# Sums of weights from the first down projection on, and the scores' biases on VectorE

## The chip, the cores and the metric

The kernel runs on one core of a Trainium2 chip. Its time is the device time of one execution in microseconds; the number compared is the median over runs. One further execution of the kernel was taken with a profiler; its trace is what the profile's rows come from.

The engines are named as in the profile: PE is TensorE (matmuls), PEld its loads of weights, DVE is VectorE, ACT is ScalarE, POOL is GpSimd, SP is SyncE, which here only issues DMAs. Each engine works through its own list of instructions in order.

## The reference: what is computed

The inputs are q, k and v of 8 batches, 8 heads, 576 positions and 64 columns in float32, and three weights. First comes attention with a window of 128 positions and a bias that falls with distance; then, for the 4608 rows of its output, two products with weights of 512 x 1536, multiplied element by element, and a product with a weight of 1536 x 512:

```python
scores = np.where(mask, scale * q @ k.T + bias, -1e9)   # mask: 0 <= rel < 128
attn = softmax(scores)
x = (attn @ v) laid out as (4608, 512)
a = x @ w_a
b = x @ w_b
out = (a * b) @ w_out
```

## The kernel before

**Precision.** Nearly every float32 operand is split into a high and a low float16 part, scaled by a power of two. A product is then three float16 matmuls (high x high, high x low, low x high). `wup` holds the split parts of the two up weights, `wdn` those of the down weight, `xs` those of a batch's x, `h` those of the hidden values.

**Batches.** The work goes by batch (0 to 7). While TensorE does the up projection (`up`, or `first_up` for batch 0) and the down projection (`down`, or `first_down`) of batch b, the attention of batch b+1 is worked through beside it. `attention()` is a generator; `Pace.along` moves it on by a share with each step of the projection, so its place is tied to the projection's steps. Attention goes by pairs of heads: load and split q and k, four banks of scores (`scores`: matmuls, an addition of the bias with its row minimum on VectorE at line 388, an exponential on ScalarE at 389), normalisation (405, 406), a transpose by DMA (411), the product with v (507).

**Plain and fast units.** The up projection of a batch goes by 12 units f of 128 hidden columns. A *plain* unit (`up_plain`) makes four results (two weights, two halves of the positions), each from two terms of 6 matmuls: 48 matmuls of 288 columns. A *fast* unit (`up_fast`) gets the same from seven products of 6 matmuls, 42 in all, after the scheme of Strassen and Winograd. It needs sums of blocks of x, and sums of blocks of the weights. `ways` says for each batch which units are plain, which come first, and which are fast. Before, batches 0 and 1 are all plain, batch 2 has 6 plain units, batch 3 has 2, and the others none.

The evictions differ too. A plain unit copies two results (ScalarE, 867) and multiplies two (VectorE, 869). A fast unit has three on ScalarE (881, 893, 899), four on VectorE (888, 904, 909, 916) and a multiplication on GpSimd (911). Both then split the hidden values (`halve`, 848 and 849).

**Sums of x.** `split_x(st, plain, fast)` splits the blocks of a batch's x, a copy on ScalarE (441) and a subtraction on VectorE (442) for each. Plain units need four blocks. Fast ones need seven, four of them after a subtraction on GpSimd (455, 458, 460, 465). A batch with both needs eight.

**Sums of weights.** `sums_of_weights()` is a generator of 25 steps. Each of the first 24 takes one half of one unit's weights: five additions on GpSimd (248 to 252). The next step commits it: two copies on ScalarE (258) and two subtractions on VectorE (260) into `wup` and `wsum`. Its scratch is unused room in `wsum` for units 0 to 7, and for units 8 to 11 it takes two of the four buffers `t` that the scores use as well. The first addition is ordered behind the last bias (`issue_after(last_bias[0].ins)`), the copies behind the last eviction of a projection. `quota` says how many steps are taken beside which steps of a batch's up and down projection. Before: 9 and 4 in batch 1, 3 and 5 in batch 2, and 4 in the down projection of batch 3. `weave` takes them in equal distances.

**The bias.** `before_scores` makes, for each pair of heads, a tile of 128 x 192: distances times the pair's scale and the heads' slopes, one `tensor_scalar` on GpSimd (365). There is one such buffer, so it is written when the pair before has read it for the last time (388).

**Order.** In the part with batch 0 the order on all engines but SyncE, and from batch 1 on the order on all engines but TensorE, is laid down beforehand by a scheduler that simulates the kernel, with earlier statements first where several are ready; `high_priority` moves the evictions up. From batch 1 on TensorE's order is that of the program.

Of the kernel before, what the change touches and what calls it, by code (L numbers as in the profile page):

```python
# [18 lines left out]
ALU = mybir.AluOpType  # L19
# [27 lines left out]
def attention_then_bilinear_ffn(ctx: ExitStack, tc: tile.TileContext, qT, kT, vP, w_a, w_b, w_out, rel, slopes2, outT):  # L47
# [187 lines left out]
    def sums_of_weights():  # L235


        spare = cycle([flat[:, n:n + 4 * P].rearrange("p (s f) -> p s f", s=4) for n in range(8 * 6 * P, 12 * 6 * P, 4 * P)])

        def place():  # L240
            return next(spare) if f < 8 else work.tile([P, 4, P], F32, tag="t", name="ws32", bufs=4)

        late = []
        for f, k in [(f, k) for f in range(NF) for k in range(2)] + [(None, None)] * 1:
            if f is not None:
                a, z = place(), place()
                with tc.issue_after(last_bias[0].ins):
                    pool.tensor_tensor(out=a, in0=wup[:, f, 0:4, 0, k, :], in1=wup[:, f, 0:4, 1, k, :], op=ALU.add)
                pool.tensor_tensor(out=z[:, 0, :], in0=a[:, 3, :], in1=a[:, 2, :], op=ALU.add)
                pool.tensor_tensor(out=z[:, 2, :], in0=a[:, 0, :], in1=a[:, 3, :], op=ALU.subtract)  # L250
                pool.tensor_tensor(out=z[:, 1, :], in0=z[:, 0, :], in1=a[:, 0, :], op=ALU.subtract)
                pool.tensor_tensor(out=z[:, 3, :], in0=a[:, 1, :], in1=z[:, 1, :], op=ALU.subtract)
            late.append((f, k, z))
            if len(late) > 1:
                g, m, x = late.pop(0)
                with tc.issue_after(last_main[0].ins):
                    for w, z in ((wup[:, g, 3:4], x[:, 0:1, :]), (wsum[:, g], x[:, 1:4, :])):
                        act.copy(w[:, :, 0, m, :], z)
                for w, z in ((wup[:, g, 3:4], x[:, 0:1, :]), (wsum[:, g], x[:, 1:4, :])):
                    vec.tensor_tensor(out=w[:, :, 1, m, :], in0=z, in1=w[:, :, 0, m, :], op=ALU.subtract)  # L260
            yield
# [100 lines left out]

    def before_scores(o, ninv):
        o.bias = work.tile([P, WIN], F32, tag="bias", name="bias")
        last_bias[0] = pool.tensor_scalar(out=o.bias, in0=rel_sb, scalar1=ninv, scalar2=sl2_sb[:, o.p:o.p + 1], op0=ALU.mult, op1=ALU.mult)  # L365
        o.mn, o.sm, o.rin = (small.tile([P, 9], F32, tag=tag, name=tag) for tag in ("mn", "sm", "rin"))
        o.n, o.parts = 0, []

# [298 lines left out]
    def attention():  # L667
# [34 lines left out]
        for i in range(n + 1):  # L702
# [53 lines left out]
            if prev and p == 0:  # L756
                states[b - 1] = st
                assert started["down"] == b - 2
                for k, _ in enumerate(split_x(st, b - 1 <= 3, b - 1 >= 2)):
                    yield i + (4.2 + 0.2 * k) / 7  # L760
            yield i + 5 / 7
            if o:
# [13 lines left out]
            prev, o = o, nxt  # L776
            yield i + 1

    states, started, first_reads, last_read, last_main, last_bias = {}, {"down": -1}, [None], [None], [None], [None]


    def new_hidden():
# [227 lines left out]


    every = list(range(NF))
    ways = [(every, [])] * 2 + [(every[6:], every[:6]), (every[10:], every[:10])] + [([], every)] * (B - 4)
    att = Pace(attention())
    spread = sums_of_weights()

    quota = [((), ()), (((8, 48, 9),), ((0, 48, 4),)), (((0, 24, 3),), ((0, 48, 5),)), ((), ((0, 48, 4),))] + [((), ())] * (B - 4)

    def first_batch():
        st = states[0]  # L1020
        weave(att.along(first_up(st, h), 49, 3.2), (weights, 0, 40, 50))
        weave(att.along(first_down(0, out_scale(st), h), 24, 5.15), (weights, 0, 12, 12))
        for _ in weights:
            pass

# [55 lines left out]
```

## Time and profile before

| | us |
|---|---|
| median of 3 runs | 991.28 (991.03 to 994.67) |
| the profiled execution | 989.81 |
| its span, first to last instruction | 988.0 |
| TensorE busy | 962.1 |
| VectorE busy | 669.0 |
| ScalarE busy | 635.6 |
| GpSimd busy | 255.3 |

The span is cut by the profiler from the first to the last instruction; the execution's own time has 1.8 us more around it. Busy time is the union of an engine's instructions. The granted clock of TensorE is 0.995 in the mean. The rows of the groups give, after the shapes and the count, the busy time in us, the mean of one instruction in ns, and the idle time of the engine before them with what ended it. In a row of the timeline the idle time and its releaser stand in brackets.

### The profile page before, as it was taken

To read this page: it belongs to the slowest core of one execution; us is meant where nothing else is said; L and a number is where in the kernel's file an instruction comes from. 1 tells how busy PE (TensorE), PEld (TensorE's weight loads), DVE (VectorE), ACT (ScalarE), POOL (GpSimd) and SP (SyncE) were. 2 spreads that over 40 slices of the span, in tenths; PEclk is the share of its full clock that TensorE was granted. 3 is DMA by queue.
4 is the path that set the end of the run, shared out by engine and by line. 5 is a ranking of instruction groups with operands and counts; after the bars stand their busy time and mean duration, and the time that the engine had idled before them with its cause. 6 is when DMAs were issued, how large, how long until landed. Compare 5 with 4: busy or idle time off the path is not lost.

```text
span 988.0 us, 23867 instructions
## 1 busy us (share of the span) xinstructions
PE 962.1 (97%) x9339; PEld 748.9 (76%) x9339; DVE 669.0 (68%) x1867; ACT 635.6 (64%) x1729; POOL 255.3 (26%) x309
## 2 busy tenths in 40 slices
PE   7899999999999999999999999999999999999998
PEld 5567777677777777777777777777777777877776
DVE  5979998668688657777778677757776576514520
ACT  5977769667676667766767766777667766413321
POOL 1211122032546313541225222211232012311100
PEclk8999999999999999999999999999999999999999
DMA  8434753664337234463345362373245432200001
GB/s 333 168 126 172 231 154 67 151 158 92 80 74 183 68 69 87 107 172 75 68 92 121 120 118 65 87 191 84 59 84 117 133 74 38 55 34 5 1 13 36
DMA packets 148432, 102.82 MB, mean 104 GB/s; under 512 B 120032, under 2 KB 128352, under 8 KB 147296
## 3 DMA queue, kind: packets, MB, share of 16 engines
q1 hardware_dynamic: 138816, 91.77, 38.2%
q10 hardware_dynamic: 9504, 9.54, 3.0%
q8 instruction: 73, 1.20, 0.5%
q14 instruction: 39, 0.32, 0.1%
HBM read 48.33 MB, written 9.44 MB: 58 GB/s over the span
## 4 chain that ended last, share of the span: by engine, by line
PE 69%; DVE 12%; ACT 7%; DMA 7%; issue 3%; POOL 1%; SPq 0%; ACTq 0%; DVEq 0%
PE ch L856 19%; PE dn_ps L952 18%; PE p L856 14%; PE up_ps L856 9%; PE x_ps L507 4%; DMA v<-in_vP 4%; PE sc_ps L384 3%; DVE phl L406 2%; PE dn_ps L818 2%; ACT t L389 1%; DVE wsum L135 1%; DVE xs L442 1%; ACT phl L405 1%; DVE wsum L134 1%; DMA qk<-in_kT 1%
## 5 line engine op out<-in xcount | busy, mean ns | idle before, releaser
L856 PEld LDWEIGHTS <-wup 128*128 128x128 f16 x3072 | 296.3, 98 | 82.0 <-issue 5.7
L952 PE MATMUL dn_ps<-h,wdn 128*128 128x288 f16 x2016 | 254.4, 286 | 0.0
L952 PEld LDWEIGHTS <-wdn 128*128 128x128 f16 x2016 | 193.9, 98 | 52.0 <-issue 0.2
L856 PE MATMUL up_ps<-xs,wup 128*128 128x288 f16 x1536 | 194.6, 286 | 1.1 <-ACT rc L867 0.8
L856 PEld LDWEIGHTS <-wsum 128*128 128x128 f16 x1152 | 111.7, 98 | 32.0 <-issue 2.5
L911 POOL TENSOR_TENSOR rc<-rc,row 128x288 f32<-128x288 f32 x64 | 62.3, 974 | 279.8 <-DVE row L909 263.9
L389 ACT ACTIVATE t<-t,mn 128x192 f32<-128x192 f32 (+2 forms) x252 | 107.2, 427 | 24.5 <-DVE mn L388 24.4
L856 PE MATMUL ch<-xs,wup 128*128 128x288 f16 x768 | 115.0, 286 | 0.5 <-ACT row L893 0.5
L856 PE MATMUL p<-xs,wup 128*128 128x288 f16 x768 | 115.1, 286 | 0.0
L406 DVE SCALAR_TENSOR_TENSOR phl<-t,rin,phl 128x192 f16<-128x192 f32 (+2 forms) x252 | 104.6, 454 | 15.3 <-ACT phl L405 15.1
L856 PE MATMUL ch<-xs,wsum 128*128 128x288 f16 x768 | 111.5, 286 | 1.1 <-ACT rc L881 1.1
L848 ACT CAST h<-rc 128x576 f16<-128x576 f32 x96 | 64.1, 668 | 69.1 <-DVE rc L916 37.2
L405 ACT ACTIVATE phl<-t,rin 128x192 f16<-128x192 f32 (+2 forms) x252 | 88.9, 425 | 25.3 <-DMA pT<-phl 12.7
L849 DVE TENSOR_TENSOR h<-rc,h 128x576 f16<-128x576 f32 x90 | 69.5, 772 | 30.5 <-ACT h L848 29.7
L388 DVE CUSTOM_DVE_ANT_0 t<-sc_ps,bias,neg 128x192 f32<-128x192 f32 (+2 forms) x216 | 73.9, 389 | 7.6 <-PE sc_ps L384 7.5
L957 ACT ACTIVATE row<-dn_ps,oi 128x288 f32<-128x288 f32 x56 | 27.6, 493 | 55.9 <-PE dn_ps L952 55.9
L893 ACT ACTIVATE row<-ch,g 128x288 f32<-128x288 f32 x64 | 31.8, 497 | 48.9 <-PE ch L856 48.9
L442 DVE TENSOR_TENSOR xs<-v,xs 128x576 f16<-128x576 f32 x52 | 47.8, 935 | 21.4 <-ACT xs L441 21.3
L888 DVE TENSOR_TENSOR rc<-p,rc 128x288 f32<-128x288 f32 x64 | 29.1, 454 | 44.3 <-PE p L856 34.7
L365 POOL TENSOR_SCALAR bias<-rel_sb,ninv,sl_sb 128x192 f32<-128x192 f32 x24 | 20.0, 832 | 147.8 <-DVE mn L388 129.8
L856 PE MATMUL p<-xs,wsum 128*128 128x288 f16 x384 | 57.5, 286 | 0.0
L436 POOL TENSOR_TENSOR xq<-xq,sq 128x576 bf16<-128x576 bf16 x22 | 29.2, 1325 | 75.7 <-ACT sq L435 75.7
(155 smaller groups left out, 1386.1 us busy)
## 6 DMA issues: line engine op xcount, KB each, us to landing
v<-in_vP SPq DMA_DIRECT2D x8, 1280.0 KB, 6.2
out<-row ACTq DMA_DIRECT2D x62, 144.0 KB, 1.8
qk<-in_qT SPq DMA_DIRECT2D x28, 288.0 KB, 4.0
qk<-in_kT SPq DMA_DIRECT2D x28, 288.0 KB, 4.4
wdn<-in_w_a SPq DMA_DIRECT2D x12, 512.0 KB, 5.1
wdn<-in_w_b SPq DMA_DIRECT2D x12, 512.0 KB, 6.1
wdn<-in_w_out SPq DMA_DIRECT2D x12, 512.0 KB, 4.6
qst<-qkh SPq DMA_DIRECT2D x24, 144.0 KB, 2.7
```

Source lines behind the costliest of these rows:

```text
L388: vec.tensor_tensor_reduce(out=t[:, c:c + w], in0=ps[:, c:c + w], in1=o.bias[:, WIN - w:WIN], scale=-0.125 if o.b == 1 else o.neg, scalar= ...
L389: act.activation(t[:, c:c + w], t[:, c:c + w], AF.Exp, bias=o.mn[:, n:n + 1], scale=-1.0, accum_out=o.sm[:, n:n + 1])
L405: act.activation(phl[:, 0, pc:pc + w], e, AF.Copy, scale=s)
L406: vec.scalar_tensor_tensor(out=phl[:, 1, pc:pc + w], in0=e, scalar=s, in1=phl[:, 0, pc:pc + w], op0=ALU.mult, op1=ALU.subtract)
L442: vec.tensor_tensor(out=xs[:, n, 1, :, :], in0=src, in1=xs[:, n, 0, :, :], op=ALU.subtract)
L507: last = pe.matmul(xp[oc // 512][64 * h:64 * h + 64, o0:o0 + w], vt[0:rows, c:c + 64], probs(pt, rows, blocks, h), start=(n == 0 and first ...
L848: act.copy(h[:, f, :, 0, :], hid)
L849: eng.tensor_tensor(out=h[:, f, :, 1, :], in0=hid, in1=h[:, f, :, 0, :], op=ALU.subtract)
L856: pe.matmul(ps[:, 0:HT], w[:, wi, k, :], xs[:, b, xi, k, :], start=(first and n == 0), stop=(last and n == len(ks) - 1), skip_group_check= ...
L893: last_read[0] = last_main[0] = act.activation(mid, ch, AF.Copy, scale=st.g)
L911: pool.tensor_tensor(out=x0, in0=x0, in1=mid, op=ALU.mult)
L952: pe.matmul(ps[:, 0:HT], wdn[:, f, wi, e * P:(e + 1) * P], h[:, f, t, hi, :], start=(m == 0 and n == 0), stop=(m == NF - 1 and n == 2))
```

## The change

- `ways`: batch 0 stays plain, batch 1 becomes 8 plain and 4 fast units, and all later batches become fast.
- `quota` and the first batch: 9 steps of the sums beside the second half of the first down projection, 10 beside the up projection of batch 1 and 6 beside its down projection. After that there are none.
- `split_x`: batch 1 is split for both kinds (eight blocks), later ones for fast units alone (seven).
- The bias is formed by VectorE. The sums' first addition is no longer ordered behind it.

```diff
@@ sums_of_weights
-                with tc.issue_after(last_bias[0].ins):
-                    pool.tensor_tensor(out=a, in0=wup[:, f, 0:4, 0, k, :], in1=wup[:, f, 0:4, 1, k, :], op=ALU.add)
+                pool.tensor_tensor(out=a, in0=wup[:, f, 0:4, 0, k, :], in1=wup[:, f, 0:4, 1, k, :], op=ALU.add)
@@ before_scores
-        last_bias[0] = pool.tensor_scalar(out=o.bias, in0=rel_sb, scalar1=ninv, scalar2=sl2_sb[:, o.p:o.p + 1], op0=ALU.mult, op1=ALU.mult)
+        vec.tensor_scalar(out=o.bias, in0=rel_sb, scalar1=ninv, scalar2=sl2_sb[:, o.p:o.p + 1], op0=ALU.mult, op1=ALU.mult)
@@ attention
-                for k, _ in enumerate(split_x(st, b - 1 <= 3, b - 1 >= 2)):
+                for k, _ in enumerate(split_x(st, b - 1 <= 1, b - 1 >= 1)):
@@
-    ways = [(every, [])] * 2 + [(every[6:], every[:6]), (every[10:], every[:10])] + [([], every)] * (B - 4)
+    ways = [(every, []), (every[4:], every[:4])] + [([], every)] * (B - 2)
-    quota = [((), ()), (((8, 48, 9),), ((0, 48, 4),)), (((0, 24, 3),), ((0, 48, 5),)), ((), ((0, 48, 4),))] + [((), ())] * (B - 4)
+    quota = [((), ()), (((8, 60, 10),), ((0, 48, 6),))] + [((), ())] * (B - 2)
@@ first_batch
-        weave(att.along(first_down(0, out_scale(st), h), 24, 5.15), (weights, 0, 12, 12))
+        weave(att.along(first_down(0, out_scale(st), h), 24, 5.15), (weights, 0, 12, 12), (spread, 12, 24, 9))
```

More of the change, by code (lines that the diff above doesn't have):

```diff
@@ L777, in attention @@
             yield i + 1
-    states, started, first_reads, last_read, last_main, last_bias = {}, {"down": -1}, [None], [None], [None], [None]
+    states, started, first_reads, last_read, last_main = {}, {"down": -1}, [None], [None], [None]
     def new_hidden():
```

## The prediction

> **What bounds the kernel now.** I read the page first, for the engines and the chain that ended last; then the timeline of TensorE, for where each batch begins and where it stood still; then the groups of instructions by line; then the stretches that the change loads. The page:
>
> ```profile
> PE 962.1 (97%) x9339; PEld 748.9 (76%) x9339; DVE 669.0 (68%) x1867; ACT 635.6 (64%) x1729; POOL 255.3 (26%) x309
> ...
> DVE  5979998668688657777778677757776576514520
> ...
> PE 69%; DVE 12%; ACT 7%; DMA 7%; issue 3%; POOL 1%; SPq 0%; ACTq 0%; DVEq 0%
> ```
>
> TensorE is busy for 97% of the span and makes 69% of the chain. A busy row alone does not say that matmuls run at their rate, so here are two merged rows of the chain, 108 and 288 matmuls of 288 columns end to end:
>
> ```profile
> 326.67 13.25 PE up_ps L856 x108
> ...
> 949.44 35.29 PE dn_ps L952 x288
> ```
>
> 13.25/108 and 35.29/288 are both 0.1225 us: with nothing in the way, that is the price of a matmul. The starts of the up projections of batches 1 to 5 on TensorE's timeline:
>
> ```profile
> 200.33 0.53 PE L856 MATMUL up_ps<-xs,wup 128*128 128x288 f16 x3
> 324.06 0.53 PE L856 MATMUL up_ps<-xs,wup 128*128 128x288 f16 x3
> 441.11 0.53 PE L856 MATMUL up_ps<-xs,wup 128*128 128x288 f16 x3
> 554.80 0.65 PE L856 MATMUL ch<-xs,wup 128*128 128x288 f16 x4
> 667.08 0.53 PE L856 MATMUL ch<-xs,wup 128*128 128x288 f16 x3
> ```
>
> The differences are 123.73, 117.05, 113.69 and 112.28 us for batches 1 to 4. By the lists in the kernel these hold 12, 6, 2 and 0 plain units, and a plain unit has 48 matmuls where a fast one has 42. From batch 2 to batch 4 six units go from plain to fast: 36 x 0.1225 = 4.4 us, and the trace has 4.77. From batch 3 to 4: 12 x 0.1225 = 1.5, and the trace has 1.41. So in this part of the kernel a removed matmul is worth its price. Where TensorE did stand still around the places that the change touches:
>
> ```profile
> 146.32 0.18 PE L103 MATMUL wtot<-c,ones 128*128 128x1 bf16 x1 [2.44 <-DVE c L102]
> ...
> 183.93 1.54 PE L507 MATMUL x_ps<-pT,vhl 128*64 128x128 f16 x42 [2.44 <-DMA pT<-phl]
> ...
> 310.65 0.18 PE L337 MATMUL qtot<-both,ones 128*128 128x2 bf16 x1 [1.17 <-DVE both L329]
> ```
>
> The stalls wait for VectorE at the end of the weights' conversion (146), for the attention's transpose in the first down projection (184), and for VectorE again in batch 1's down projection (311). How full VectorE is there, by stretches (length, then PE, PEld, DVE, ACT and POOL busy):
>
> ```profile
> 80.00:140.00 60.00, 60.00 (x538) 45.96 (x537) 58.97 (x126) 41.62 (x103) 13.25 (x14) 1.00 0.60 186
> ...
> 165.00:200.30 35.30, 32.87 (x362) 25.32 (x360) 19.92 (x66) 21.88 (x62) 4.82 (x5) 1.00 0.69 147
> ...
> 255.00:282.00 27.00, 26.59 (x259) 21.29 (x257) 20.08 (x53) 19.02 (x54) 14.00 (x23) 1.00 0.34 75
> 282.00:311.00 29.00, 27.83 (x292) 21.43 (x290) 24.96 (x72) 20.20 (x60) 15.47 (x16) 1.00 0.48 97
> ```
>
> VectorE is full from 80 to 140 (58.97 of 60), half empty in the first down projection (19.92 of 35.30), at 74% at the end of batch 1's up projection and at 86% right behind it. GpSimd is idle in the first down projection (4.82 of 35.30).
>
> **The change, part by part.** *Matmuls.* Plain units fall from 12 + 6 + 2 = 20 to 8, all in batch 1. Twelve units give up 6 matmuls each: 72 x 0.1225 = **-8.8 us**, of which 24 matmuls in batch 1 (2.9), 36 in batch 2 (4.4) and 12 in batch 3 (1.5). These are on the bounding engine.
>
> *Batches 2 and 3.* They become what batch 4 is, but for the stage of their attention. They lose all of their 12 steps of sums, and split 7 blocks of x instead of 8. By the differences above, the stalls that go beside the matmuls are 4.77 - 4.4 and 1.41 - 1.5, together **-0.3 us** (bounds -1.5 and 0: neither batch can lose more idle time than the 1.17 us kind of stall that the trace shows around them).
>
> *The evictions that a fast unit adds.* Rows of the groups, by line (busy us, mean ns of one):
>
> ```profile
> L869 DVE SCALAR_TENSOR_TENSOR rc<-rc,g,up_ps 128x288 f32<-128x288 f32 x40 | 20.2, 507 | 3.0 <-PE up_ps L856 2.8
> ...
> L888 DVE TENSOR_TENSOR rc<-p,rc 128x288 f32<-128x288 f32 x64 | 29.1, 454 | 44.3 <-PE p L856 34.7 <-ACT rc L881 5.9 <-ACT phl L405 3.4
> L904 DVE TENSOR_TENSOR rc<-ch,rc 128x288 f32<-128x288 f32 x64 | 29.2, 456 | 10.5 <-PE ch L856 10.1
> L909 DVE SCALAR_TENSOR_TENSOR row<-p,g,row 128x288 f32<-128x288 f32 x64 | 32.8, 512 | 6.5 <-PE p L856 6.1
> L916 DVE SCALAR_TENSOR_TENSOR rc<-rc,g,ch 128x288 f32<-128x288 f32 x64 | 32.7, 511 | 23.6 <-PE ch L856 23.4
> L911 POOL TENSOR_TENSOR rc<-rc,row 128x288 f32<-128x288 f32 x64 | 62.3, 974 | 279.8 <-DVE row L909 263.9 <-ACT rc L881 13.2 <-ACT phl L405 2.7
> ```
>
> A plain unit costs VectorE 2 x 0.507 = 1.01 us, a fast one 0.454 + 0.456 + 0.512 + 0.511 = 1.93: 0.92 us more for each of the 12, and GpSimd 0.97 more. In batches 2 and 3 this is the load that batch 4 carries already, behind a full TensorE, so nothing. In batch 1 it is 4 x 0.92 = 3.7 us, all in the last 28 of 60 steps, since plain units come first.
>
> *The sums of weights.* One step is five additions on GpSimd, two copies on ScalarE and two subtractions on VectorE; the views of lines 248, 249 and 260 give min/median/max:
>
> ```profile
> L248 POOL TENSOR_TENSOR wsum<-wup x16: 1149/1160/1667, 213.1 to 357.1; 128x512 f32<-128x512 f16 x16
> L249 POOL TENSOR_TENSOR wsum<-wsum x16: 452/484/1041, 217.0 to 358.4; 128x128 f32<-128x128 f32 x16
> ...
> L260 DVE TENSOR_TENSOR wup<-wsum,wup x16: 277/292/1279, 230.8 to 406.3; 128x128 f16<-128x128 f32 x16
> L260 DVE TENSOR_TENSOR wsum<-wsum x16: 544/558/1503, 231.1 to 406.7; 128x384 f16<-128x384 f32 x16
> ```
>
> With the other three short additions taken as the one shown, a step is 1.16 + 4 x 0.48 = 3.1 us of GpSimd and 0.29 + 0.56 = 0.85 of VectorE. Their number stays 24 (a 25th only commits the last); only the place moves. Nine go into the second half of the first down projection: 28 us of GpSimd, which has 30 idle there, and 7.7 of VectorE, which has 15.4. There too go four more splits of batch 1's x and the four subtractions before them:
>
> ```profile
> L442 DVE TENSOR_TENSOR xs<-v,xs 128x576 f16<-128x576 f32 x52 | 47.8, 935 | 21.4 <-ACT xs L441 21.3
> ...
> L458 POOL TENSOR_TENSOR v<-v 128x576 f32<-128x576 f32 x6 | 8.4, 1408 | 46.4 <-ACT v L420 46.4
> ```
>
> That is 4 x 0.94 = 3.7 us of VectorE and 4 x 1.41 = 5.6 of GpSimd. VectorE then has 19.9 + 7.7 + 3.7 = 31.3 of 35.3 us to do. GpSimd overflows a little into batch 1, which harms nobody: the first fast unit comes behind 32 plain steps of 12 matmuls, 32 x 12 x 0.1225 = 47 us later. What can harm is an in-order queue: the addition of squares (GpSimd), the copies of the commits (ScalarE) and the exponentials stand in one line, and the transpose at 184 is already late. Bounds for this stretch: 0 when the lists slip past each other, and 5 us when half of the 7.7 + 3.7 us of VectorE come ahead of the transpose. I take **+0.7 us**, nearer to nothing because both engines had near half of the stretch free.
>
> *The end of batch 1's up projection* (255 to 282 now). It gets shorter by 24 x 0.1225 = 2.9 us, so 24.1. VectorE has 20.1 now, with three and a half commits; with six it gets 2.5 x 0.85 = 2.1 more, 3.7 for the fast units and 0.4 for a bias: 26.3. That is more than the stretch holds, by 2.2 us, and the next one (24.96 of 29.00, six sums in the whole down projection instead of four, one split fewer) cannot take much of it; its stall at 311 shows that attention had no slack left. Bounds: 0, when the plain stage ahead runs commits early; 6 us, when the 2.2 comes together with the whole 3.7 of the fast units. I take **+1.8 us**.
>
> *The biases.* 28 of them move from GpSimd to VectorE. The trace has no such instruction on VectorE; beside its row on GpSimd stand the nearest ones on VectorE, two scalars on one column, and one scalar on 288 columns out of PSUM:
>
> ```profile
> L365 POOL TENSOR_SCALAR bias<-rel_sb,ninv,sl_sb 128x192 f32<-128x192 f32 x24 | 20.0, 832 | 147.8 <-DVE mn L388 129.8 <-ACT rc L867 18.0
> ...
> L964 DVE TENSOR_SCALAR oi<-g,smin,so 128x1 f32<-128x1 f32 x8 | 2.2, 271 | 0.2
> L823 DVE TENSOR_SCALAR row<-dn_ps,oi 128x288 f32<-128x288 f32 x3 | 1.5, 510 | 0.0
> ```
>
> So between 0.27 and 0.51 us; by width 0.27 + 192/288 x 0.24 = 0.43, and I take 0.41. Most of them lie under a full TensorE. Two do not: this timeline of GpSimd puts two biases into the stretch where VectorE is full and TensorE then waits for it at 146.
>
> ```profile
> 82.64 0.43 POOL L365 TENSOR_SCALAR bias<-rel_sb,sl_sb 128x192 f32<-128x192 f32 x1 [0.30 <-DVE mn L388]
> 112.48 0.86 POOL L365 TENSOR_SCALAR bias<-rel_sb,sl_sb 128x192 f32<-128x192 f32 x1 [0.60 <-DVE mn L388]
> ```
>
> 2 x 0.41 = **+0.8 us** (0.5 to 1.0). What the move frees is GpSimd's queue: its bias had to wait for VectorE's last read of the one bias buffer, and the sums were ordered behind it. On VectorE that wait is the engine's own order. The view of line 365 lists nobody who waited for it, so nothing is gained directly.
>
> *The sum:* -8.8 - 0.3 + 0.7 + 1.8 + 0.8 = -5.8 us. The span of 988.0 becomes 982.2, the profiled execution's 989.81 becomes 984.0. The median of the runs, 991.28, lies 1.5 above that execution; with the same distance I predict **985.5 us**.
>
> **A rule against it.** When VectorE and GpSimd add at the same time, both are slow. VectorE's timeline and GpSimd's at 300, and the group of that VectorE instruction over the whole run:
>
> ```profile
> 300.83 3.64 DVE L406 SCALAR_TENSOR_TENSOR phl<-t,rin,phl 128x192 f16<-128x192 f32 x3 [0.52 <-ACT phl L405]
> ...
> 300.40 2.38 POOL L248 TENSOR_TENSOR wsum<-wup 128x512 f32<-128x512 f16 x2
> ...
> L406 DVE SCALAR_TENSOR_TENSOR phl<-t,rin,phl 128x192 f16<-128x192 f32 x196 | 88.5, 493 | 6.1 <-ACT phl L405 6.0
> ```
>
> Three instructions took 3.64 us, 1.2 each instead of the mean of 0.49, beside two first additions of 1.2 each. The Trainium skill says why (SBUF — State Buffer, Who interferes with whom): the two engines share a pair of ports, held for a whole instruction; a VectorE instruction with two inputs in SBUF, or one such as a scalar operation in its two-port mode, and a GpSimd instruction that reads SBUF wait for each other in full. The two rows agree with it.
>
> **Rivals.** (A) *Forecast*: the matmuls' price less stalls of some 3 us. (B) *Clean saving*: the list order absorbs the three stall terms; -8.8 - 0.3 and half a bias term leave about -8.7, 982.6 us. For it: batches 2 to 4 show the full price. Against: VectorE at 26.3 of 24.1. (C) *Given back*: VectorE becomes the bound from 165 to 311, where sums on GpSimd, now free to run beside everything, stretch VectorE's two-input work as at 300. All 24 first additions would stand there, where 13 stood by `quota`; each of the 11 more costs up to 1.2 - 0.5 = 0.7 us of VectorE's time, 7.7 us. With all of it on the path in place of my 0.7 + 1.8: -8.8 - 0.3 + 0.8 + 7.7 = -0.6, 990.7 us, no change. For it: the rows at 300. Against: it happened at 300 beside a stall of only 1.17 us. By the port rule alone (C) would be the likeliest; I give less, since the same additions run in both kernels. (D) *Slower*: the commits stand on the chain. In first down and batch 1, VectorE and ScalarE run their lists in order, TensorE's order is fixed by hand in batch 1, and a score's product waits at its place. The work added from 165 to 324 is 9 x 0.85 + 4 x 0.94 + 7 x 0.41 + 4 x 0.92 + 3 x 0.85 = 20.5 us of VectorE. If all of it reached TensorE: -8.8 - 0.3 + 0.8 + 20.5 = +12, 1003.5 us. It decides from 13.3 us on the path (two thirds), where the sum is +5. Against: VectorE has 15.4 us free in the first down projection alone. (E) *It doesn't do what it says*: the sums come no earlier, because their copies wait for ScalarE's output evictions, and the first fast unit waits; 47 us of slack speak against it.
>
> **How the numbers follow.** About 0.5% (5 us) is what a measurement of this kernel can tell from no change; the bounds are 986.3 and 996.2. A 0.42 and B 0.16 make faster 0.58. C 0.31 and E 0.03 make no change 0.34. D has 0.08. The range of 8 in 10 is 981.0 (B with 1.5 us of stalls gone) to 991.0 (C). A's own is 982.9 to 987.5.
>
> **What would show it.** Right: line 856 with 72 matmuls fewer; batches 2 and 3 at about 112.3 us each; batch 1 at 122 to 124 us; the up projection of batch 1 starting 1 to 2 us later than 200.33; biases on VectorE at 0.41; GpSimd's sums starting at about 165. Wrong: batch 1 over 128 us, new waits of TensorE at line 337 or 384 on VectorE above 3 us, or batch 1 beginning after 205, would mean (C) or (D). Batch 1 under 121 would mean (B).

## The result: slower by 1.2%, and the profile after

The changed kernel takes **1004.18 us** (median of 6 runs, 1002.91 to 1005.76), beside 992.03 for the kernel before on the same chip (988.85 to 994.67). The ratio is 1.0124, 95% interval 1.0104 to 1.0145. Forecast were 985.5 us and a range up to 991.0: wrong in size and in sign.

The page of the changed kernel, the rows that answer to those of before:

```profile
span 1002.8 us, 23788 instructions
...
PE 957.4 (95%) x9267; PEld 742.8 (74%) x9267; DVE 700.7 (70%) x1921; ACT 642.2 (64%) x1743; POOL 260.6 (26%) x297
...
PE 68%; DVE 16%; DMA 6%; ACT 6%; issue 2%; POOL 0%; SPq 0%; ACTq 0%; DVEq 0%; POOLq 0%
```

And the groups of the biases on VectorE (busy us, mean ns):

```profile
L364 DVE TENSOR_SCALAR bias<-rel_sb,ninv,sl_sb 128x192 f32<-128x192 f32 x24 | 9.8, 407 | 0.2
...
L364 DVE TENSOR_SCALAR bias<-rel_sb,sl_sb 128x192 f32<-128x192 f32 x4 | 1.2, 308 | 0.0
```

Three things are in them. TensorE has 72 matmuls fewer (9339 to 9267), as the lists say, yet its busy time falls by 4.7 us where 72 x 0.1225 = 8.8 were expected. Its idle time rises from 988.0 - 962.1 = 25.9 to 1002.8 - 957.4 = 45.4 us. That is 19.5 us, and 19.5 - 4.7 is the 14.8 us by which the span grew. The missing 4.1 us of busy time fit a lower granted clock: its mean over the span is 0.991, and was 0.995, and 0.4% of 957 us is 3.8. And VectorE is busy for 31.7 us more. The counted work explains 28 biases (11.0 us), twelve fast units at 0.92 (11.0) and two more splits at 0.94 (1.9), together 23.9; the count of instructions fits as well (28 + 24 + 2 = 54 = 1921 - 1867). The other **7.8 us belong to no added instruction**: existing ones got longer. VectorE's share of the chain rose from 12 to 16%.

Where the time went by batch, from TensorE's timeline of the changed kernel (the same five starts as before; behind line 247 the numbers are one lower than before):

```profile
210.87 0.53 PE L855 MATMUL up_ps<-xs,wup 128*128 128x288 f16 x3
346.52 0.65 PE L855 MATMUL ch<-xs,wup 128*128 128x288 f16 x4
458.37 0.53 PE L855 MATMUL ch<-xs,wup 128*128 128x288 f16 x3
569.73 0.53 PE L855 MATMUL ch<-xs,wup 128*128 128x288 f16 x3
681.56 0.53 PE L855 MATMUL ch<-xs,wup 128*128 128x288 f16 x3
```

| from one up projection's start to the next, us | before | after | measured | forecast |
|---|---|---|---|---|
| batch 0 (with first down) | 144.42 | 157.60 | +13.2 | +1.5 |
| batch 1 | 123.73 | 135.65 | +11.9 | -1.1 |
| batch 2 | 117.05 | 111.85 | -5.2 | -4.8 |
| batch 3 | 113.69 | 111.36 | -2.3 | -1.4 |

Batch 0's first up projection began 2.65 us earlier, and all behind batch 3 comes to -0.1, which closes the 14.8. Not all of the +13.2 is a loss: 22 of TensorE's matmuls stood ahead of that start before and stand behind it now, some 2.9 us (batch 0 of "gate behind the squares", below, has them too, and TensorE busy for 140.84 us where it was 137.93). So it is in every kernel below that has the bias on VectorE, and in none that has it on GpSimd. Like for like, batch 0 is some 10.3 us longer, and batch 1 begins 10.5 us later. Batches 2 and 3 gained what was forecast, or a little more. All that went wrong lies ahead of 346 us, in two about equal halves. TensorE's waits there, on its timeline:

```profile
191.96 2.77 PE L506 MATMUL x_ps<-pT,vhl 128*64 128x128 f16 x42 [5.30 <-DMA pT<-phl]
...
227.61 1.63 PE L855 MATMUL up_ps<-xs,wup 128*128 128x288 f16 x12 [1.53 <-DVE rc L868]
...
287.56 0.27 PE L383 MATMUL sc_ps<-qkh,qst 128*64 128x192 f16 x2 [2.10 <-DVE mn L387]
...
301.04 1.30 PE L855 MATMUL ch<-xs,wsum 128*128 128x288 f16 x6 [1.74 <-DVE rc L903]
...
333.10 0.18 PE L336 MATMUL qtot<-both,ones 128*128 128x2 bf16 x1 [2.25 <-DVE oi L965]
```

The first is the stall of before at 183.93, now 5.30 us instead of 2.44. The same 42 matmuls behind it then take 2.77 us where they took 1.54: they run at little more than half the rate. The others wait for VectorE, beginning in the plain part of batch 1, where the prediction saw 47 us of slack.

Three stretches of these two batches have the granted clock (the last figure but two) at half; the kernel before has 1.00 over both batches:

```profile
188.70:195.60 6.90, 3.64 (x47) 3.05 (x48) 4.45 (x16) 3.60 (x9) 0.85 (x1) 0.51 0.27 81
287.70:291.10 3.40, 3.40 (x21) 2.06 (x18) 3.15 (x11) 3.40 (x12) 1.77 (x2) 0.51 0.05 11
301.40:304.80 3.40, 3.40 (x29) 2.31 (x28) 3.40 (x7) 1.18 (x2) 3.21 (x5) 0.50 0.57 107
```

TensorE is busy for 10.44 us in them. At half the rate that is an estimated 5.2 us of the loss in batches 0 and 1. Over the whole span it shows as 4.1 us, because ahead of batch 0 the changed kernel's clock is the higher one (0.97 for 0.91).

Now the first down projection in detail. First two stretches of the kernel before (length, then PE, PEld, DVE, ACT and POOL busy, granted clock):

```profile
153.50:165.00 11.50, 11.50 (x99) 8.52 (x97) 11.30 (x32) 11.50 (x31) 1.31 (x1) 1.00 0.31 59
...
153.50:200.30 46.80, 44.37 (x458) 33.85 (x456) 31.21 (x97) 33.38 (x91) 6.13 (x6) 1.00 0.60 125
```

and on its VectorE timeline the five instructions of one normalisation:

```profile
168.20 1.53 DVE L406 SCALAR_TENSOR_TENSOR phl<-t,rin,phl 128x64 f16<-128x64 f32 x5
```

The answering stretch of the changed kernel (the same matmuls, 459 to 458, up to batch 1's start):

```profile
152.40:210.90 58.50, 46.80 (x459) 35.26 (x458) 52.62 (x109) 40.34 (x111) 39.52 (x46) 0.94 0.45 95
```

Its first addition of the sums on GpSimd's timeline, and the same five instructions on VectorE's:

```profile
156.35 1.60 POOL L247 TENSOR_TENSOR wsum<-wup 128x512 f32<-128x512 f16 x1 [7.26 <-DVE wdn L232]
...
172.14 4.06 DVE L405 SCALAR_TENSOR_TENSOR phl<-t,rin,phl 128x64 f16<-128x64 f32 x5
```

The sums do not start at about 165, as forecast, but at 156.35, where VectorE was full already: 11.30 of 11.50 us before. From there on the five instructions take 4.06 us instead of 1.53. VectorE has 12 instructions more in the stretch and 21.4 us more busy time, and the stretch is 11.7 us longer: all of batch 0's loss.

### The profile page after: what moved, and what is told of

Its sections match the earlier page's. It is cut to its first block, busy times and chain, and to the rows that moved or that the text cites. A ratio compares the mean times of both kernels' runs of the same rounds, so it can differ in the third digit from the quotient of the medians.

```text
span 1002.8 us, 23788 instructions
## 1 busy us (share of the span) xinstructions
PE 957.4 (95%) x9267; PEld 742.8 (74%) x9267; DVE 700.7 (70%) x1921; ACT 642.2 (64%) x1743; POOL 260.6 (26%) x297
## 4 chain that ended last, share of the span: by engine, by line
PE 68%; DVE 16%; DMA 6%; ACT 6%; issue 2%; POOL 0%; SPq 0%; ACTq 0%; DVEq 0%; POOLq 0%
PE ch L855 22%; PE dn_ps L951 17%; PE p L855 16%; PE up_ps L855 6%; PE x_ps L506 3%; DVE phl L405 3%; PE sc_ps L383 3%; DMA v<-in_vP 2%; DMA pT<-phl 2%; DVE xs L441 2%; DVE t L387 1%; ACT t L388 1%; ACT phl L404 1%; DVE wsum L134 1%; DVE wdn L232 1%
## 5 line engine op out<-in xcount | busy, mean ns | idle before, releaser
L855 PEld LDWEIGHTS <-wup 128*128 128x128 f16 x2784 | 268.2, 98 | 81.3 <-issue 11.9
L910 POOL TENSOR_TENSOR rc<-rc,row 128x288 f32<-128x288 f32 x76 | 78.2, 1029 | 406.6 <-DVE row L908 363.1
L855 PEld LDWEIGHTS <-wsum 128*128 128x128 f16 x1368 | 133.4, 98 | 39.9 <-issue 4.5
L855 PE MATMUL p<-xs,wup 128*128 128x288 f16 x912 | 136.6, 286 | 1.2 <-ACT rc L898 1.2
L855 PE MATMUL ch<-xs,wup 128*128 128x288 f16 x912 | 136.6, 286 | 1.1 <-ACT row L892 1.0
L855 PE MATMUL ch<-xs,wsum 128*128 128x288 f16 x912 | 134.0, 287 | 2.5 <-DVE rc L903 1.7
L855 PE MATMUL up_ps<-xs,wup 128*128 128x288 f16 x960 | 123.1, 286 | 4.4 <-ACT rc L866 2.3
L441 DVE TENSOR_TENSOR xs<-v,xs 128x576 f16<-128x576 f32 x54 | 60.4, 1126 | 17.8 <-ACT xs L440 17.5
L915 DVE SCALAR_TENSOR_TENSOR rc<-rc,g,ch 128x288 f32<-128x288 f32 x76 | 38.8, 510 | 25.4 <-PE ch L855 25.3
L506 PE MATMUL x_ps<-pT,vhl 128*64 128x128 f16 (+2 forms) x1176 | 44.6, 232 | 7.1 <-DMA pT<-phl 6.9
```

The costliest lines, as they stand in the source:

```text
L441: vec.tensor_tensor(out=xs[:, n, 1, :, :], in0=src, in1=xs[:, n, 0, :, :], op=ALU.subtract)
L506: last = pe.matmul(xp[oc // 512][64 * h:64 * h + 64, o0:o0 + w], vt[0:rows, c:c + 64], probs(pt, rows, blocks, h), start=(n == 0 and first ...
L855: pe.matmul(ps[:, 0:HT], w[:, wi, k, :], xs[:, b, xi, k, :], start=(first and n == 0), stop=(last and n == len(ks) - 1), skip_group_check= ...
L910: pool.tensor_tensor(out=x0, in0=x0, in1=mid, op=ALU.mult)
L915: vec.scalar_tensor_tensor(out=x1, in0=x1, scalar=st.g, in1=ch, op0=ALU.mult, op1=ALU.mult)
```

## The experiments

Two explanations fit these traces. *The overlap*: additions on GpSimd, no longer ordered behind a bias (I call that order the gate), start early and stretch VectorE's instructions. *The work*: the commits, the biases and the fast units fill VectorE and ScalarE, and the additions are harmless. The ratios stand against the kernel before on the same chip (its medians were 991.15, 990.4 and 991.83 us beside the three groups below). Differences of ratios are given in percentage points. Each trace is one execution; where it lay 3 us or more from the median of its kernel, this is said.

### Each part alone

**Bias and gate alone.** The kernel before with the bias on VectorE and the gate gone; sums, units and splits as before:

```diff
-                with tc.issue_after(last_bias[0].ins):
-                    pool.tensor_tensor(out=a, ...)
+                pool.tensor_tensor(out=a, ...)
-        last_bias[0] = pool.tensor_scalar(out=o.bias, ...)
+        vec.tensor_scalar(out=o.bias, ...)
```

> The kernel before with one part of the change alone: the biases on VectorE, and the sums' first addition no longer ordered behind a bias. Units, splits and sums stay as before. Theory 1 (the added VectorE work of the early sums and splits stands on the chain) and theory 2 (the additions on GpSimd stretch VectorE's two-input work while both run) both have nothing moved into the first down projection here: within 3 us of the kernel before. Theory 3 (the freed gate or the 28 biases on VectorE are the damage): at least 997 us.

Measured: 999.44 us, ratio 1.0074 (1.0055 to 1.0094). The part that the prediction had costed at +0.8 and "nothing" costs 7 us by itself. GpSimd's timeline says why:

```profile
156.87 1.59 POOL L247 TENSOR_TENSOR wsum<-wup 128x512 f32<-128x512 f16 x1 [7.26 <-DVE wdn L232]
```

In this kernel the lists still put the first sums beside batch 1's up projection, at its step 8. The scheduler takes them forward by some 56 us (213.14 before), past that place: GpSimd is idle there, and nothing holds them.

**The sums alone.** The changed kernel with the bias on GpSimd and the gate as before (the diff above, backwards):

> The changed kernel with the biases back on GpSimd and the sums' first addition ordered behind the last bias again; the 9, 10 and 6 steps, the units and the splits as changed. Theories 1 and 2: the damage stays, 999 to 1006 us. Theory 3: 984 to 990 us, the 72 matmuls' 8.8 us less a little.

Measured: 1002.63 us, ratio 1.0107 (1.0081 to 1.0134). Its sums and batch starts, on the timelines of GpSimd and TensorE:

```profile
172.85 3.61 POOL L248 TENSOR_TENSOR wsum<-wup 128x512 f32<-128x512 f16 x3
...
204.32 0.41 PE L856 MATMUL up_ps<-xs,wup 128*128 128x288 f16 x2
...
340.24 0.53 PE L856 MATMUL ch<-xs,wup 128*128 128x288 f16 x3
```

With the gate the sums start 16 us later, and batch 1 begins at 204.32 instead of 210.87; but batch 1 itself takes 135.92 us, as in the changed kernel. So the early, dense lists hurt too. The two parts do not add up (0.74 + 1.07 is more than the 1.24 points of both): both bring sums into the first down projection. With the rest of the change in place, the gate and the bias together are worth 0.17 points, which is within the noise.

**No additions.** The changed kernel without the five additions of a step; the sums are a constant, and the commits stay:

```diff
-                a, z = place(), place()
-                (five additions and subtractions of a and z on GpSimd)
+                _, z = place(), place()
+                pool.memset(z, 0.001)
```

> The changed kernel with the five additions of each step on GpSimd left out and one memset of the result in their place, which reads nothing; the copies and subtractions that commit it stay (the weights' sums are then constants, so the output is not the reference's). Theory 2 (the two engines' instructions hold each other up): first down projection back to 3 us of its length before, under 993 us. Theory 1 (the commits and splits by themselves): at least 999 us.

Measured: 988.69 us, ratio 0.9968 (0.9956 to 0.9981). TensorE's starts of batches 1 and 2:

```profile
199.67 0.41 PE L851 MATMUL up_ps<-xs,wup 128*128 128x288 f16 x2
...
328.76 0.41 PE L851 MATMUL ch<-xs,wup 128*128 128x288 f16 x2
```

Without the additions 1.56 points are gone, all of the loss and more. (One write of GpSimd per step is left of its five additions.) Batch 0 gets 10.8 us shorter than in the changed kernel (146.82 for 157.60), batch 1 6.6 (129.09 for 135.65). GpSimd's additions, an engine 26% busy and on 0% of the chain, are the greatest single cause.

**Batch 1 plain, no sums in first down.** The changed kernel with all units of batch 1 plain, with the splits of x that go with it, and the sums beside batch 1 alone; the gate stays away:

```diff
-    ways = [(every, []), (every[4:], every[:4])] + [([], every)] * (B - 2)
+    ways = [(every, [])] * 2 + [([], every)] * (B - 2)
-    quota = [((), ()), (((8, 60, 10),), ((0, 48, 6),))] + ...
+    quota = [((), ()), (((8, 48, 13),), ((0, 48, 12),))] + ...
-        weave(att.along(first_down(...), 24, 5.15), (weights, 0, 12, 12), (spread, 12, 24, 9))
+        weave(att.along(first_down(...), 24, 5.15), (weights, 0, 12, 12))
```

> The changed kernel with no sums beside the first down projection: batch 1 all plain and split in four blocks, 13 steps of the sums beside its up projection and 12 beside its down projection, batches 2 to 7 all fast. 48 matmuls fewer than before, 5.9 us. If the damage is made in the first down projection (theories 1 and 2 there): 986 to 991 us. If it is made wherever the sums stand close together: 995 us or more, with batch 1 over 125 us.

Measured: 998.59 us, ratio 1.0075 (1.0051 to 1.0098). Batch 0 still takes 156.14 us: the list no longer asks for a sum there, and the sums come all the same. Without the gate the list's place doesn't bind. Batch 1 takes 132.65 us, 8.9 more than before with the same matmuls, so dense sums cost there as well. (This trace lies 3.0 us above its median.)

### The gate or the bias, and what the commits cost

**Gate behind VectorE's bias.** The bias on VectorE, and the first addition ordered behind that bias:

```diff
-        last_bias[0] = pool.tensor_scalar(out=o.bias, ...)
+        last_bias[0] = vec.tensor_scalar(out=o.bias, ...)
```

> The kernel before with the biases on VectorE, and the sums' first addition still ordered behind the last bias, now VectorE's. Theory gate (the run with the biases alone took 8 us more because the freed additions went ahead to 157 us, beside the end of the weights' conversion): the sums stay in batch 1, 990 to 994 us. Theory bias (28 instructions more on VectorE): 997 us or more.

Measured: 997.94 us, ratio 1.0072 (1.005 to 1.0093). It decides nothing between gate and bias. GpSimd's timeline shows that the order held nothing back; the sums start as early as without it:

```profile
155.12 1.60 POOL L248 TENSOR_TENSOR wsum<-wup 128x512 f32<-128x512 f16 x1 [7.27 <-DVE wdn L232]
```

`issue_after` orders an instruction only behind one of its own engine, so naming VectorE's bias binds nothing on GpSimd. The kernel is "bias and gate alone" once more, and its ratio is the same (1.0072 and 1.0074).

**Gate alone.** The kernel before, bias on GpSimd, and only the gate taken away: the first diff without its last two lines.

> The kernel before with the gate alone gone: biases stay on GpSimd, the sums' first addition is ordered behind nothing. Theory gate: sums start at about 157 us and the time is 996 to 1001 us. Theory bias: 989 to 994 us.

Measured: 1001.17 us, ratio 1.0108 (1.0093 to 1.0123). One ordering gone, and the kernel is 10.8 us slower. Its stretch up to batch 1:

```profile
156.40:210.30 53.90, 47.00 (x458) 35.27 (x456) 38.41 (x98) 31.86 (x89) 22.64 (x24) 0.94 0.56 115
```

On its timelines of VectorE and TensorE, the same five instructions, the transpose's product, and batch 1's start:

```profile
173.47 4.76 DVE L405 SCALAR_TENSOR_TENSOR phl<-t,rin,phl 128x64 f16<-128x64 f32 x5
...
191.64 0.64 PE L506 MATMUL x_ps<-pT,vhl 128*64 128x128 f16 x8 [4.91 <-DMA pT<-phl]
...
210.31 0.41 PE L855 MATMUL up_ps<-xs,wup 128*128 128x288 f16 x2
```

VectorE has 98 instructions, 97 before, and is busy for 38.41 us instead of 31.21. GpSimd has 24 instructions instead of 6. No commit, no fast unit and no bias is in it. The five instructions at 168 take 4.76 us for 1.53; the transpose behind the normalisation is late, TensorE waits 4.91 us for it and comes back at a lower clock (0.94 over the stretch). The stretch is 7.1 us longer. By batches, 0 to 3, this kernel takes 9.1, 1.5, -0.3 and 1.4 us more than the one before: nearly all of the loss is in the first. Not all of the 9.1 comes from the sums, however: from 148.7 to 155.5 us, ahead of the first sum at 158.14, the granted clock is 0.50 with TensorE busy for 6.02 us, an estimated 3.0 us. The two kernels without the gate that have the bias on VectorE lost 0.74 and 0.72%, so the gate is worth 7 to 11 us.

**No commits.** The changed kernel with the subtractions of the commits on VectorE (line 259) replaced by constants that GpSimd writes:

```diff
-                    vec.tensor_tensor(out=w[:, :, 1, m, :], in0=z, in1=w[:, :, 0, m, :], op=ALU.subtract)
+                    pool.memset(w[:, :, 1, m, :], 0.0)
```

> The changed kernel with VectorE's two subtractions of each commit left out and the low parts of the sums set to zero by GpSimd (so the output is less exact than the reference's). The additions stay. Theory 1 (VectorE's own added work is what reaches TensorE): 24 x 0.85 to 1.2 us of VectorE are gone, 989 to 995 us. Theory 2 (the additions stretch VectorE's other instructions): 998 to 1003 us, and the first down projection of batch 0 stays 5 us or more longer than before.

Measured: 996.64 us, ratio 1.0054 (1.0034 to 1.0073). That lies between the two expectations, 0.70 points less than the changed kernel and about half of what the additions gave. The place differs as well: batch 1 takes 126.18 us for 135.65, while batch 0 stays at 156.39 for 157.60. The commits cost in batch 1, the additions in the first down projection and less in batch 1. Of the 9.5 us in batch 1, some 3.4 are the clock, which stays at 1.00 there in this trace.

**Gate and batch 1 plain.** The kernel of the fourth experiment with the gate and GpSimd's bias:

> The kernel before, biases and gate untouched, with 13 and 12 steps of the sums in batch 1, which stays plain, and all batches from 2 on fast (48 matmuls fewer, 5.9 us). Differs from the run with no sums in the first down projection by the gate and the place of the bias alone. Theory gate: batch 0 is as before (batch 1 starts at 200 to 201 us), batches 2 and 3 at 112 us each, batch 1 at 124 to 129 us: 985 to 991 us, a candidate for a faster kernel. If dense sums are the damage by themselves: batch 1 over 130 us, 993 us or more.

Measured: 999.20 us, ratio 1.0089 (1.0065 to 1.0112). Batch 0 with the gate and without sums takes 146.65 us, but batch 1 with all of them 133.42; 24 sums beside one batch are too many, with plain units too. (This trace lies 3.2 us above its median.) Its batches 0 and 1 by stretches:

```profile
57.10:203.70 146.60, 140.79 (x1349) 106.77 (x1347) 119.51 (x308) 103.22 (x265) 25.27 (x29) 0.98 0.54 153
203.70:337.20 133.50, 125.98 (x1206) 97.19 (x1205) 107.82 (x286) 92.24 (x269) 86.14 (x117) 0.96 0.48 106
```

and two stalls on its TensorE timeline; the first is used at the end of this document, the second waits for VectorE's row minimum of a score:

```profile
185.74 2.16 PE L507 MATMUL x_ps<-pT,vhl 128*64 128x128 f16 x42 [2.43 <-DMA pT<-phl]
...
273.65 0.37 PE L384 MATMUL sc_ps<-qkh,qst 128*64 128x192 f16 x2 [4.34 <-DVE mn L388]
```

### The mechanism, and what is left

**Gate behind the squares.** The kernel before with the bias on VectorE, and the first addition ordered behind GpSimd's last addition of squares:

```diff
-                with tc.issue_after(last_bias[0].ins):
+                with tc.issue_after(last_sq[0].ins):
-        last_bias[0] = pool.tensor_scalar(out=o.bias, ...)
+        vec.tensor_scalar(out=o.bias, ...)
-            pool.tensor_tensor(out=st.xq, in0=st.xq, in1=sq, op=ALU.add)
+            last_sq[0] = pool.tensor_tensor(out=st.xq, in0=st.xq, in1=sq, op=ALU.add)
```

> The kernel before with the biases on VectorE and the sums' first addition ordered behind the last addition of squares, which is GpSimd's own, so that the sums cannot go ahead of batch 1's attention (in the runs with the biases alone they went ahead to 157 us, also where they were to follow VectorE's bias). Theory gate: 28 biases on VectorE cost under 2 us in sum, sums from about 190 us on, 989 to 993 us. Theory bias: 996 us or more.

Measured: 992.07 us, ratio 1.0006 (0.9994 to 1.0019). The bias on VectorE costs nothing once the sums are held. The view of its line (min/median/max), the first sums on GpSimd, and batch 1's start:

```profile
L365 DVE TENSOR_SCALAR bias<-rel_sb,ninv,sl_sb x24: 366/376/1278, 169.8 to 804.9; 128x192 f32<-128x192 f32 x24
...
189.07 3.92 POOL L248 TENSOR_TENSOR wsum<-wup 128x512 f32<-128x512 f16 x3
...
198.16 0.41 PE L856 MATMUL up_ps<-xs,wup 128*128 128x288 f16 x2
```

The sums come at 189, and batch 0 takes 145.07 us, 144.42 before.

**Gate alone, memsets for additions.** The kernel of "gate alone", its five additions replaced by five memsets of the same tiles and shapes. GpSimd still has an early queue, but reads nothing in it:

```diff
-                (five additions and subtractions of a and z on GpSimd)
+                pool.memset(a, 0.001)
+                for s in (0, 2, 1, 3):
+                    pool.memset(z[:, s, :], 0.001)
```

> The kernel before with the gate gone, as in the run with the gate alone gone (1001 us), but with five memsets of the same shapes in place of the five additions of every step: they write and read nothing (sums are constants, so the output is not the reference's). Theory 2 (a reading GpSimd instruction holds VectorE's two-input instructions up): batch 1 starts again at 199 to 202 us, VectorE's stretched instructions are gone, 986 to 991 us. Rival (GpSimd's queue is merely full, and its squares and splits come late): 996 us or more.

Measured: 989.83 us, ratio 0.9982 (0.9969 to 0.9995). Its stretch up to batch 1:

```profile
154.70:201.50 46.80, 44.46 (x459) 33.90 (x458) 32.76 (x97) 33.92 (x92) 17.15 (x34) 1.00 0.60 128
```

The first memsets and a later subtraction of hidden values on GpSimd's timeline, and the five instructions on VectorE's:

```profile
157.90 1.69 POOL L247 MEMSET wsum<- 128x512 f32 x3 [5.94 <-DVE wdn L232]
...
168.21 2.47 POOL L846 TENSOR_TENSOR h<-rc,h 128x576 f16<-128x576 f32 x1
...
169.46 2.56 DVE L403 SCALAR_TENSOR_TENSOR phl<-t,rin,phl 128x64 f16<-128x64 f32 x5
```

GpSimd is as early and has more instructions than with the additions (34 to 24), and VectorE is busy for 32.76 us, not 38.41; the stretch is 46.80 long, as before. The five instructions still take 2.56 us for 1.53: beside them runs the subtraction of line 846, which reads, and which is in all of these kernels. The groups of VectorE within this stretch, of the kernel before, of "gate alone" and of this one, show which instructions suffered: the normalisation has two inputs in SBUF, the score's row minimum reads its scores from PSUM. The six row minima shown are those that stood beside additions in "gate alone".

```profile
L406 DVE SCALAR_TENSOR_TENSOR phl<-t,rin,phl 128x192 f16<-128x192 f32 (+2 forms) x20 | 6.9, 396 | 3.2 <-ACT phl L405 3.2
...
L388 DVE CUSTOM_DVE_ANT_0 t<-sc_ps,bias 128x192 f32<-128x192 f32 x6 | 1.9, 353 | 0.8 <-PE sc_ps L380 0.8
```

In "gate alone":

```profile
L405 DVE SCALAR_TENSOR_TENSOR phl<-t,rin,phl 128x192 f16<-128x192 f32 (+2 forms) x20 | 11.3, 611 | 4.7 <-ACT phl L404 4.7
...
L387 DVE CUSTOM_DVE_ANT_0 t<-sc_ps,bias 128x192 f32<-128x192 f32 x6 | 1.9, 349 | 0.1
```

With memsets for the additions:

```profile
L403 DVE SCALAR_TENSOR_TENSOR phl<-t,rin,phl 128x192 f16<-128x192 f32 (+2 forms) x20 | 7.9, 446 | 3.0 <-ACT phl L402 3.0
...
L385 DVE CUSTOM_DVE_ANT_0 t<-sc_ps,bias 128x192 f32<-128x192 f32 x6 | 1.9, 350 | 0.0
```

The same twenty normalisations take 6.9, 11.3 and 7.9 us, the same six row minima 1.9 in all three. So the mere number of GpSimd's early instructions does not cost the 10.8 us; additions that read SBUF beside VectorE's two-input instructions cost most of it. One part is left open: a memset is also shorter than an addition (17.15 us for all 34 instructions, 22.64 for 24), so reading and duration were not fully separated.

**No sums at all.** The changed kernel without additions and without VectorE's subtractions of the commits:

> The changed kernel with neither the additions nor VectorE's part of the commits (memsets by GpSimd in their places; the output is not the reference's). What is left of the change: 72 matmuls fewer, two splits of x more, 12 fast units' evictions and the biases on VectorE. With the additions and commits as the whole damage: 981 to 985 us. If the evictions and splits cost by themselves: 986 us or more.

Measured: 986.38 us, ratio 0.9957 (0.9941 to 0.9973). Even with no price on the sums the new order of units gains 0.43%, 4.3 us of the 9.1 that the prediction's matmuls and batches 2 and 3 promised. The other 4.8 are lost neither to the additions nor to VectorE's part of the commits. TensorE's starts of batches 1 and 2, with a stall of the new batch 1 between them:

```profile
199.10 0.53 PE L851 MATMUL up_ps<-xs,wup 128*128 128x288 f16 x3
...
218.32 12.12 PE L851 MATMUL up_ps<-xs,wup 128*128 128x288 f16 x84 [2.43 <-ACT rc L862]
...
327.52 0.41 PE L851 MATMUL ch<-xs,wup 128*128 128x288 f16 x2
```

Batch 1 takes 128.42 us; 24 matmuls fewer than before would be 120.8. (This trace lies 3.8 us above its median.) Additions (1.56 points), commits (0.70) and both together (1.67) also show how the two overlap: once the additions are gone, the commits are worth 0.11, which is within the noise.

**A smaller step.** In search of a faster kernel: that of before with the sums done by the end of batch 2 and the last two plain units of batch 3 made fast, 12 matmuls and one split fewer:

```diff
-    ways = [(every, [])] * 2 + [(every[6:], every[:6]), (every[10:], every[:10])] + [([], every)] * (B - 4)
+    ways = [(every, [])] * 2 + [(every[6:], every[:6])] + [([], every)] * (B - 3)
-    quota = [..., (((0, 24, 3),), ((0, 48, 5),)), ((), ((0, 48, 4),))] + [((), ())] * (B - 4)
+    quota = [..., (((0, 66, 5),), ((0, 48, 7),))] + [((), ())] * (B - 3)
```

> The kernel before, biases and gate untouched, with the last four steps of the sums drawn from batch 3's down projection into batch 2 (5 beside its up and 7 beside its down projection) and batch 3 all fast: 12 matmuls and one split fewer, 1.5 us. If a thin spread of the sums carries them at no cost: 988 to 991 us beside 990 to 992 before. If every sum beside a projection costs TensorE what the runs so far show (about 0.6 us a step): no gain, 991 to 994 us.

Measured: 994.69 us, ratio 1.0032 (1.0020 to 1.0044). Batch 2 with twelve sums instead of eight takes 119.57 us for 117.05, more than the 1.5 us that the matmuls could give. (This trace has batch 3 at 113.83 for 113.69, so even they did not show.) No kernel that does all of the work came out faster than the one before.

## Why the prediction was wrong, step by step

**The step that failed is an overlap.** The sum took GpSimd's additions as filling idle room, at no cost to VectorE beside them. The runs showed the opposite: without the additions the changed kernel takes 988.69 us, with them 1004.18. The error stands in three terms.

**The gate, costed at nothing.** The prediction wrote that the sums were "ordered behind" the bias and that "nothing is gained directly" from freeing them. It asked who waits for the bias, and gave what the freed instructions would do next no price in its sum; only the rival (C) had them run beside everything. Taking it away alone costs 10.8 us (some 7 where the bias moved as well); 9.1 of them are in batch 0, beside the changed kernel's 10.3 like for like. It is enough for the loss, but not needed: with the gate and GpSimd's bias back, "the sums alone" still lose 1.07%.

**First down projection, +0.7 with bounds of 0 and 5.** Batch 0 became some 10 us longer. Two errors. The free time of VectorE was a mean from 165 to 200, though the full stretch ended just there; the sums started 9 us ahead of it. And the added work was summed at undisturbed durations, 31.3 of 35.3 us, while GpSimd's share was taken as room that costs VectorE nothing. The upper bound counted lists that slip, not instructions that get longer.

**End of batch 1, +1.8 with bounds of 0 and 6.** Batch 1 came out 135.65 - 120.8 = 14.8 us above its matmuls' price. Some 3.4 us of it are the clock. Removing the commits takes 9.5 us, the additions 6.6 (with overlap, and each with a part of the clock's 3.4), and 5.4 us of extra idle time stay with no sums at all (7.85 us, 2.42 before). The prediction looked at the last 28 of 60 steps; the waits begin at 227 already, in the plain part, for an eviction of VectorE. A late first batch does not explain it: in "gate alone" batch 1 begins as late, at 210.31, and takes only 1.5 us more than before, and in "the sums alone" it begins at 204.32 and takes 135.92. How the 14.8 divide between commits, additions and the fast units' own work stays open.

**Right:** the price of a matmul and batches 2 and 3 (-6.2 forecast, -7.5 measured); the bias on VectorE (0.41 forecast, median 0.37 measured), harmless in "gate behind the squares"; the 72 matmuls. The signs named as wrong ahead of time (batch 1 over 128 us, beginning after 205) both appeared. The waits at 336 and 383 (337 and 384 before) did not pass 3 us; the longest one was the transpose's.

**The rivals.** The outcome has the size of (D), 1003.5, which had a chance of 0.08, but not its cause alone: the commits are the smaller part. The mechanism of the larger part is that of (C). Its price, 7.7 us of VectorE's time, is near the 7.8 us that belong to no added instruction in the changed kernel, but by luck: (C) took 0.7 us for each of 11 first additions, and in "gate alone" 18 additions, only six of them first ones, made VectorE 7.2 us longer. (C) put all of it on TensorE's path, and there it was (a stretch 7.1 us longer); that the clock would fall as well, neither (C) nor the sum had. The two rivals were held as alternatives, and both hold at once: additions that run early make the first batch late, commits, additions and fast units crowd batch 1, and the clock takes some 5 us in the two. They don't simply add, though: with both prices the prediction's sum is +19.9, and +12.2 was measured. The reason given against (C), that "it happened at 300 beside a stall of only 1.17 us", came from a stretch with VectorE at 86%, not at 98%.

**The port rule** (the Trainium skill, SBUF — State Buffer, Who interferes with whom) was quoted and then outweighed with "the same additions run in both kernels". They do, at other places. The measurements agree with the rule: beside additions that read, twenty two-input instructions of VectorE took 11.3 us instead of 6.9, and six that take their scores from PSUM stayed at 1.9. The page also says that a GpSimd instruction which only writes does not hold up such a VectorE instruction; the stretch with memsets, no longer than before, agrees. (The memsets are shorter too, as said.)

## What to carry to other kernels

When an ordering is removed, ask first where the freed instructions will go: here the scheduler moved them 56 us forward on an idle engine, and an order that looks like a by-product may be what keeps them out of a full stretch of a neighbour. Work on an idle GpSimd is priced by what VectorE does beside it, in the fullest stretch and not the mean one. Two rivals with different mechanisms that act on the same chain can hold at once; such an outcome needs a time and a chance of its own.

## What was not expected of the hardware

**How much the additions stretch.** 18 more instructions on GpSimd made VectorE's 98 longer by 7.2 us, 0.4 for each of the 18, and one group of five three times as long (1.53 to 4.76); 28 more, mostly memsets, cost 1.5 us (31.21 to 32.76).

**A short stall may or may not bring a lower clock.** In the kernel before, TensorE stood 2.44 us ahead of the 42 matmuls at 183.93, which took 1.54 us. In "gate and batch 1 plain" it stood 2.43 us ahead of the same 42, which took 2.16. Over all of batch 0 that kernel has less idle time (146.60 - 140.79 = 5.81) than the one before, with the same 1349 matmuls:

```profile
55.90:200.30 144.40, 137.91 (x1349) 104.66 (x1348) 119.77 (x310) 102.69 (x264) 24.98 (x30) 1.00 0.55 154
```

Its 6.49 us of idle time went with a granted clock of 1.00, the other's 5.81 with 0.98, and 2.9 us more of busy time. The Trainium skill (TensorE: Matmul & The Clock Gate, Part 1: The HAM clock gate) has the clock fall to half after at least one idle window of about 3.4 us. The stall of 5.30 us in the changed kernel agrees; the one of 2.43 us does not by its length alone. What differs is where the two short stalls lie. In each of the fourteen traces here the granted clock changes only at multiples of 3.41 us from its other changes. Two steps of that grid around the stall, first in the kernel before, then in "gate and batch 1 plain":

```profile
179.50:182.90 3.40, 1.99 (x21) 1.29 (x19) 0.97 (x8) 1.57 (x7) 0.00 (x0) 1.00 1.07 258
182.90:186.30 3.40, 2.37 (x50) 2.16 (x51) 1.94 (x6) 2.33 (x6) 0.00 (x0) 1.00 0.03 11
...
183.00:186.40 3.40, 0.97 (x26) 0.75 (x24) 1.19 (x9) 0.62 (x3) 0.00 (x0) 1.00 0.55 175
186.40:189.80 3.40, 3.40 (x37) 2.54 (x34) 3.34 (x10) 3.40 (x11) 0.00 (x0) 0.51 0.00 0
```

In the first, a border of the grid cuts the stall, and no step has more than 1.4 us of idle time. In the second, one step holds all of its 2.43 us, and the next is at half. Between 60 and 980 us, the fourteen traces have twenty steps at full clock with more than 2.0 us of idle time, and half the clock follows each of them; where it was below 1.8 us, it follows none. So here it decides where on the grid a short stall falls, and part of what a stall costs is luck. The share of the clock in the loss, an estimated 5.2 us in batches 0 and 1, has no experiment that holds it fixed.
